# A fused attention and two-layer-MoE kernel: the first pair's q and k turned by TensorE, and the first loads and rows in another order

## The chip, the cores and the metric

The kernel runs on one core of a Trainium2 chip. A core has engines that each work through their own list of instructions in order: TensorE (PE; its weight loads are shown as PEld), VectorE (DVE), ScalarE (ACT), GpSimd (POOL) and SyncE (SP), whose list here holds nearly all the DMA issues. An instruction that waits for a semaphore holds up everything behind it on its engine. The metric is the time of one execution on the device in microseconds (us); lower is better.

## The reference

Batch 4, 8 heads, 576 rows (S), head size 64 (D); 2304 tokens in all, model width 512, hidden width 2048.

```python
scores = scale * np.matmul(q, k.transpose(0, 1, 3, 2))
thresh = np.max(scores, axis=-1, keepdims=True) - tau
scores = np.where(scores >= thresh, scores, -1e9)
attn = np.exp(scores - np.max(scores, axis=-1, keepdims=True))
attn = attn / (np.sum(attn, axis=-1, keepdims=True) + 1e-09)
x = np.matmul(attn, v)            # then heads side by side: (2304, 512)
h = x @ w_in                      # first MoE, 512 -> 2048
P = a[0] + a[1]*h + a[2]*h**2 + a[3]*h**3
Q = 1.0 + abs(b[0])*abs(h) + abs(b[1])*h**2
x = (P / (Q + 1e-6)) @ w_out      # 2048 -> 512
h = x @ w_in2                     # second MoE
g = np.where(h >= 1, h, np.where(h <= -1, 0.0, (h + 1)**2 / 4))
return g @ w_out2
```

The MoE weights come as 64-bit floats.

## The kernel before, in words

Every product is made from float16 pairs: a number is written as a high part plus a low part (`split`, L204), and a product takes three float16 matmuls. Weights come from DRAM as pairs of 32-bit words; `as_float` (L220) puts them together on DVE with three instructions of 128x1024 each (L228, L229, L230), PE finds their size (`pg`), and `split` scales them on ACT (L217), casts them on ACT (L208) and subtracts on POOL (L212). That is done in "halves": `make_half` for the 16 halves of the first MoE, whose result stays in SBUF in the chunks `wc` and is also written to `scratch`; `stage_half` for the 16 halves of the second MoE, which go to `scratch` only. The raw words of a half are the tile `rw` (two buffers, 1 MB each: `rw_0_0` is the first half of `w_in`, `rw_0_1` the first of `w_out`), the joined ones `wt` (three buffers).

Time falls into stages. First comes the **attention of batch 0** (`first_attention`), with nothing to overlap it but the halves. Heads go in four pairs. `prep_pair` loads a pair's q and k into `rqk` (one buffer), finds their size (square on ACT, `mqke` through PE, `qkr_s` on DVE), splits them into `qk`, turns `qk` by a DMA transpose into `qkT` (q and k with D and low part on the partitions), and makes `kT2`, the same k with its high and low halves crosswise, by two more DMAs from `kT`. For pairs 2 and 3 q and k are turned by one transpose each. `first_v` loads v (ten DMAs). `row_max` makes the scores once to find each row's maximum (PE `sm`, DVE `mx`, L524), cuts the maxima into three pieces (`pcs`), turns them on PE (`pmr`) and copies them to `mrow` (ACT, L560). Then nine steps for each pair (`transposed`) make the scores again, keys on the partitions, with the maximum subtracted by a third matmul (PE `st`), mark what lies under the threshold (ACT `low`, L581), subtract that on PE, take the exponential (ACT `et`, L584) and multiply by v (PE `pv`, L593). `divide` ends a pair (ACT `rd`, DVE `d` L607) and writes `xT`. The row maxima of the next pair run between the nine steps of this one.

Then the **dense steps** run: for each batch a phase of 24 steps of the first MoE and one of 24 of the second (three blocks of 192 tokens, eight chunks). `first_product` makes `ph` (L843), `rational` or `quadratic` works on it (ACT L724 to L733; DVE L726, L727, L728, L731, L737 in the first MoE; only L789 and L790 in the second), and `second_product` adds to `acc` (L857). The other halves of the second MoE and the attention of batches 1 to 3 (`attention`, row by row: PE `s`, DVE `sc` L422, `nt` L424 and `e` L384, ACT, POOL `hl`, a DMA transpose to `eT`, PE `pv` L410) are laid beside the dense steps.

The order on each engine is not the order of the code: a list scheduler places instructions by a priority and by its own reckoning of when things are ready. The code sets priorities only, with `at(when)`; unit n of 53 of `first_attention` is at `36 * n / 53 - 40`, half number k at `2.4 * k - 40`, dense step n at n, and the attention of batch 1 is spread over steps 18 to 50. A `yield` in `first_attention` ends a unit.

## Time and profile before

| | |
|---|---|
| three timed runs | 1240.43, 1245.51 (median), 1251.01 us |
| the profiled execution, its own time | 1242.5 us |
| its span, first to last instruction | 1240.7 us |
| busy over the span: PE, DVE, ACT, POOL | 88%, 79%, 68%, 44% |
| mean granted TensorE clock | 0.959 |

The shares are averages over stages with different limits; the rows further down cut the span into these stages. A group of rows gives busy time, the mean duration of one instruction, and the idle time of the engine just before, with what ended it.

### The profile page before, as it was taken

The numbers are of one execution on the slowest core, as the hardware profiler recorded it, in microseconds if no ns is written. First come the engines' busy times: TensorE is split into PE (matmuls) and PEld (weight loads), VectorE is DVE, ScalarE is ACT, GpSimd is POOL, SyncE is SP. The second block draws the span as 40 slices with busy tenths as digits, with TensorE's granted clock in tenths as the row PEclk, the third lists the DMA queues.
The fourth block names the chain that finished last, engine by engine and source line by source line (L and its number), as shares of the span: only waits on it lengthen the run. The fifth ranks groups of instructions, "written<-read, shape, count | busy, mean of one in ns | idle before, by whom it ended". The sixth has DMA issues, their size and how long they took to land.

```text
span 1240.7 us, 31727 instructions
## 1 busy us (share of the span) xinstructions
PE 1091.9 (88%) x12618; PEld 984.5 (79%) x12618; DVE 977.1 (79%) x2353; ACT 842.9 (68%) x1533; POOL 543.0 (44%) x700
## 2 busy tenths in 40 slices
PE   2787788588799999999888998998899999999998
PEld 1444455488688888899788898998788989999997
DVE  7767887899997777799997776899996768896431
ACT  2477776779785677777875776887766767775332
POOL 3424545675673556421464555223563653222221
PEclk9797898799899999999999999999999999999999
DMA  7656676734447465923596539513993478007000
GB/s 209 230 169 217 218 258 205 240 116 120 108 136 234 68 125 116 249 73 92 144 238 131 110 69 245 140 49 68 243 192 69 86 167 221 14 1 259 16 14 27
DMA packets 220341, 176.40 MB, mean 142 GB/s; under 512 B 182048, under 2 KB 193312, under 8 KB 212000
## 3 DMA queue, kind: packets, MB, share of 16 engines
q1 hardware_dynamic: 220192, 174.36, 52.7%
q8 instruction: 99, 1.62, 0.5%
q14 instruction: 50, 0.41, 0.1%
HBM read 106.83 MB, written 21.50 MB: 103 GB/s over the span
## 4 chain that ended last, share of the span: by engine, by line
PE 35%; DVE 19%; DMA 9%; ACT 6%; POOL 6%; issue 6%; SPq 1%; DVEq 0%; ACTq 0%; POOLq 0%
PE ph L843 15%; PE acc L857 15%; DMA eT<-hl 7%; POOL hl L395 3%; DVE e L384 2%; PE pv L410 2%; DVE t L731 2%; DVE t L726 2%; DVE sc L422 2%; DVE t L737 1%; DMA qkT<-qk 1%; DVE t L728 1%; POOL gg L212 1%; DVE t L727 1%; ACT hl L392 1%
## 5 line engine op out<-in xcount | busy, mean ns | idle before, releaser
L857 PE MATMUL acc<-gg,wc 128*128 128x192 f16 x4608 | 427.6, 247 | 9.8 <-POOL gg L212 6.4
L843 PEld LDWEIGHTS <-wc 128*128 128x128 f16 x4608 | 389.8, 99 | 37.4 <-issue 20.8
L857 PEld LDWEIGHTS <-wc 128*128 128x128 f16 x4608 | 383.4, 98 | 13.3 <-issue 12.0
L212 POOL TENSOR_TENSOR gg<-t,gg 128x384 f16<-128x384 f32 x192 | 193.3, 1008 | 380.0 <-ACT gg L208 330.0
L843 PE MATMUL ph<-xT,wc 128*128 128x192 f16 x2304 | 220.2, 253 | 29.7 <-DVE t L728 21.2
L843 PE MATMUL ph<-yT,wc 128*128 128x192 f16 x2304 | 215.9, 247 | 1.0 <-DVE rk_f L160 0.6
L395 POOL TENSOR_TENSOR hl<-e,hl 128x256 f16<-128x256 f32 x216 | 154.3, 735 | 0.0
L208 ACT CAST gg<-t 128x384 f16<-128x384 f32 x192 | 97.0, 508 | 68.8 <-DVE t L790 34.7
L789 DVE SCALAR_TENSOR_TENSOR t<-t,c 128x384 f32<-128x384 f32 x96 | 64.0, 667 | 77.3 <-ACT t L788 77.0
L384 DVE SCALAR_TENSOR_TENSOR e<-sc,nt,e 128x576 f32<-128x576 f32 x108 | 96.2, 891 | 31.9 <-ACT e L383 31.3
L393 POOL TENSOR_TENSOR hl<-e,hl 128x64 f16<-128x64 f32 x108 | 43.3, 401 | 145.0 <-ACT hl L392 141.4
L788 ACT ACTIVATE t<-ph,c 128x384 f32<-128x384 f32 x96 | 64.0, 667 | 51.6 <-PE ph L843 51.2
L383 ACT ACTIVATE e<-sc,nt,con 128x576 f32<-128x576 f32 x108 | 93.4, 865 | 7.4 <-POOL hl L395 1.3
L410 PE MATMUL pv<-v,eT 128*128 128x65 f16 (+3 forms) x1680 | 70.1, 194 | 26.8 <-DMA eT<-hl 26.6
L422 DVE TENSOR_SCALAR_CACHE_REDUCE sc<-s 128x576 f32<-128x576 f32 x108 | 80.9, 749 | 13.5 <-PE s L377 12.7
L410 PEld LDWEIGHTS <-eT 128*128 128x128 f16 (+1 forms) x1680 | 62.2, 100 | 36.1 <-DMA eT<-hl 33.8
L724 ACT ACTIVATE t<-ph,sc 128x384 f32<-128x384 f32 x96 | 55.2, 575 | 51.5 <-PE ph L843 50.0
L392 ACT CAST hl<-e 128x576 f16<-128x576 f32 x108 | 72.0, 668 | 25.9 <-DVE e L384 25.3
L731 DVE SCALAR_TENSOR_TENSOR t<-t,ka,t 128x384 f32<-128x384 f32 x96 | 70.1, 730 | 11.1 <-ACT t L730 10.8
L729 ACT ACTIVATE t<-t,lc 128x384 f32<-128x384 f32 x96 | 67.9, 708 | 15.4 <-DVE t L726 15.0
L212 POOL TENSOR_TENSOR wc<-wt,wc 128x256 f16<-128x256 f32 x64 | 55.3, 897 | 46.1 <-ACT wc L208 46.1
L212 POOL TENSOR_TENSOR wh<-wt,wh 128x256 f16<-128x256 f32 x64 | 59.7, 961 | 33.0 <-ACT wh L208 28.9
(231 smaller groups left out, 1901.7 us busy)
## 6 DMA issues: line engine op xcount, KB each, us to landing
wc<-scratch SPq DMA_DIRECT2D x56, 1024.0 KB, 5.8
rw<-in_moe_w_in_dram SPq DMA_DIRECT2D x16, 1024.0 KB, 5.7
rw<-in_moe_w_out_dram SPq DMA_DIRECT2D x16, 1024.0 KB, 5.1
scratch<-wc SPq DMA_DIRECT2D x8, 1024.0 KB, 5.1
scratch<-wh SPq DMA_DIRECT2D x16, 512.0 KB, 3.6
rqk<-in_q_dram SPq DMA_DIRECT2D x16, 256.0 KB, 3.6
rqk<-in_k_dram SPq DMA_DIRECT2D x16, 256.0 KB, 3.0
kT<-qkT SPq DMA_DIRECT2D x28, 144.0 KB, 2.5
```

What stands on the lines that cost most here:

```text
L208: A.copy(hi, src)
L212: G.tensor_tensor(lo[:, p], src[:, p], hi[:, p], op=ALU.subtract)
L383: A.activation(e, s, AF.Exp, bias=nb, scale=con[:, 0:1])
L384: V.scalar_tensor_tensor(e, s, th, e, op0=ALU.is_ge, op1=ALU.mult)
L392: A.copy(hi, e)
L395: G.tensor_tensor(lo_w[:, p], e[:, whole][:, p], hi[:, whole][:, p], op=ALU.subtract)
L410: T.matmul(pv[rows, 0:w], eT[:, c, cols], vv[:, h * NT + x if x < NT else H * NT + h, at : at + w], start=(n == 0), stop=(n == len(blocks) ...
L422: V.tensor_scalar(s, banks[:, 0:S], 1.0, -LARGEST, op0=ALU.mult, op1=ALU.max, accum_out=mx)
L729: A.activation(r, u, AF.Ln, bias=lc[:, 1:2], scale=lc[:, 0:1])
L731: V.scalar_tensor_tensor(s, s, ka[:, 0:1], r, op0=ALU.add, op1=ALU.mult)
L843: last = T.matmul(ph[:, f, :], w[:, wx, kt, f * P : (f + 1) * P], rhs, start=(n == 0), stop=(n == 3 * KT - 1))
L857: T.matmul(dst, w[:, wx, f, d * P : (d + 1) * P], gg[:, gx, f, :], start=(i == 0 and f == 0 and n == 0 and d % 2 == 0), stop=(i == NCH - 1 ...
```

## The change

Six edits, all in the attention of batch 0 and the first loads:

1. A new function `turned` replaces the DMA transpose and the two crosswise DMAs of pair 0. PE multiplies each of the 18 128x128 blocks of `qk` by an identity (`qk_t`, in the PSUM banks of `s`, `acc` and `ph1`); ACT copies q to `qT` and one half of k crosswise to `kT2`, DVE copies k to `kT` and the other half to `kT2`.
2. For pair 0 the low parts of q and k are made on DVE (`on_vector`) in place of POOL, and the high parts directly by ACT.
3. `tau`, `a`, `b` and the first two weight loads (`rw_0_0`, `rw_0_1`) are issued by ACT in place of SP.
4. The `mrow` copies of pair 0 go from ACT to DVE, with a PSUM bank for each.
5. Pairs 2 and 3 are prepared after the first and after the sixth step (`PREPARE`) in place of ahead of all steps.
6. The halves' priority goes from `- 40` to `- 39.5`.

```diff
--- before.py
+++ after.py
@@ -35,6 +35,7 @@
 N_TEMP, N_POLY, N_WT, N_WH, N_GG, N_ROW, N_SC = 5, 3, 3, 2, 4, 3, 2
 
 
+PREPARE = 1, 6
 ATTENTION = {1: (18, 50), 2: (60, 100), 3: (108, 147)}
 WEIGHTS = (0, 20)
 
@@ -112,11 +113,11 @@
         return sp.tile([P, n], F32, name=name, tag=f"s{n}_{tag}", bufs=4 if tag in ("mx", "nt") else 2)
 
     tau_t = small(1, "tau_t", True)
-    Q.dma_start(tau_t, tau.partition_broadcast(P))
+    A.dma_start(tau_t, tau.partition_broadcast(P))
     a_t = small(4, "a_t", True)
-    Q.dma_start(a_t, coef_a.partition_broadcast(P))
+    A.dma_start(a_t, coef_a.partition_broadcast(P))
     b_t = small(2, "b_t", True)
-    Q.dma_start(b_t, coef_b.partition_broadcast(P))
+    A.dma_start(b_t, coef_b.partition_broadcast(P))
 
 
 
@@ -238,7 +239,7 @@
         else:
             raw = rp.tile([P, NF, DM * words], raw_type, name=f"rw{m}_{i}_1", tag="rw")
             src = w_out_dram[m][i * CF : (i + 1) * CF, :].rearrange("(f p) d -> p f d", p=P)
-        Q.dma_start(raw, src)
+        (A if m == 0 and i == 0 else Q).dma_start(raw, src)
         name = f"{m}_{i}_{x}"
         src = as_float(raw.rearrange("p a b -> p (a b)"), name)
         hi, lo = dst[:, 0:E], dst[:, E : 2 * E]
@@ -314,6 +315,22 @@
                 split(to[:, :, 0:D], to[:, :, D + 1 : 2 * D + 1], raw[:, n0:n1], s_x[b], on_vector)
         return vv
 
+    def turned(qk, qT, kT, kT2):
+        last = ps_1.tile([P, 512], F32, name="qk_t8", tag="ph1")
+        for x in (1, 0):
+            most = ps_2.tile([P, 1024], F32, name=f"qk_t{x}", tag="s" if x else "acc")
+            for c in range(C):
+                dst = most[:, c * P : (c + 1) * P] if c < C - 1 else last[:, x * P : (x + 1) * P]
+                T.matmul(dst, qk[:, x, c], ident16, start=True, stop=True)
+            for src, c0, c1 in ((most, 0, C - 1), (last[:, x * P : (x + 1) * P], C - 1, C)):
+                src = src.rearrange("p (c s) -> p c s", s=P)
+                if x == 0:
+                    A.copy(qT[:, c0:c1], src)
+                else:
+                    V.tensor_copy(kT[:, c0:c1], src)
+                    A.copy(kT2[0:D, c0:c1], src[D : 2 * D])
+                    V.tensor_copy(kT2[D : 2 * D, c0:c1], src[0:D])
+
     def prep_pair(b, pr, on_vector=True):
         raws = rp.tile([P, 2, C + 1, D], F32, name=f"rqk{b}_{pr}", tag="rqk", bufs=1)
         raw = raws[:, :, 0:C, :]
@@ -340,9 +357,12 @@
             split(qk[:, x, :, 0:D], qk[:, x, :, D : 2 * D], raw[:, x], s[:, x : x + 1], on_vector)
         if b > 0 or pr < 2:
             qkT = ap.tile([P, 2 * C, P], F16, name=f"qkT{b}_{pr}", tag="qkT")
-            Q.dma_start_transpose(out=qkT, in_=qk.rearrange("p x c d -> p (x c d)"))
             qT, kT = qkT[:, 0:C], qkT[:, C : 2 * C]
             kT2 = ap.tile([P, C, P], F16, name=f"kT2{b}_{pr}", tag="kT2")
+            if b == 0 and pr == 0:
+                turned(qk, qT, kT, kT2)
+                return con, qT, kT, kT2
+            Q.dma_start_transpose(out=qkT, in_=qk.rearrange("p x c d -> p (x c d)"))
         else:
             qT, kT, kT2 = (ap.tile([P, C, P], F16, name=f"{x}{b}_{pr}", tag="eT" if pr == 2 else "hl", bufs=N_ROW)
                            for x in ("qT", "kT", "kT2"))
@@ -553,11 +573,11 @@
             V.tensor_scalar(pcs[:, x], m, 1.0 / PIECES[x], None, op0=ALU.mult)
             if x < 2:
                 V.scalar_tensor_tensor(m, pcs[:, x], -PIECES[x], m, op0=ALU.mult, op1=ALU.add)
-        for c0, c1 in ((0, NT), (NT, 2 * NT), (2 * NT, n)):
-            pm = ps_1.tile([P, 512], F32, name=f"pmr{pr}_{c0}", tag="ph0")
+        for x, (c0, c1) in enumerate(((0, NT), (NT, 2 * NT), (2 * NT, n))):
+            pm = ps_1.tile([P, 512], F32, name=f"pmr{pr}_{c0}", tag="ph0" if pr else ("ph0", "ph1", "pv")[x])
             for c in range(c0, c1):
                 T.matmul(pm[0:3, (c - c0) * P : (c - c0 + 1) * P], pcs[:, :, c], ident16, start=True, stop=True)
-            A.copy(mrow[0:3, c0 * P : c1 * P], pm[0:3, 0 : (c1 - c0) * P])
+            (A.copy if pr else V.tensor_copy)(mrow[0:3, c0 * P : c1 * P], pm[0:3, 0 : (c1 - c0) * P])
         yield
 
     def transposed(pr, ab, t, data, n):
@@ -618,7 +638,7 @@
 
     def first_attention():
 
-        pairs = [prep_pair(0, 0, False)]
+        pairs = [prep_pair(0, 0)]
         yield
         vv = first_v()
         xT[0] = [xp.tile([P, 2 * KT, TB], F16, name=f"xT0_{j}", tag="xT", bufs=NB) for j in range(NB)]
@@ -629,9 +649,6 @@
         pairs.append(prep_pair(0, 1, False))
         yield
         for _ in row_max(0, *pairs[0][1:], mrows[0]):
-            yield
-        for pr in range(2, NP):
-            pairs.append(prep_pair(0, pr, False))
             yield
         n = 0
         for pr in range(NP):
@@ -658,6 +675,9 @@
                     next(rows, None)
                 n += 1
                 yield
+                if n in PREPARE:
+                    pairs.append(prep_pair(0, len(pairs), False))
+                    yield
             for f in held:
                 f()
             divide(pr, x, d)
@@ -870,7 +890,7 @@
         with at(36 * n / N_FIRST - 40):
             next(att)
         while halves and len(halves) * N_FIRST > 2 * NCH * (N_FIRST - 1 - n):
-            with at(2.4 * (2 * NCH - len(halves)) - 40):
+            with at(2.4 * (2 * NCH - len(halves)) - 39.5):
                 i, x = halves.pop(0)
                 make_half(0, i, x, chunks[0, i], False)
```

What the scheduler makes of it, at three places. First, DVE at the start of the program, where the size of q and k (`mqke_0`) becomes the scale `qkr_0_s`. Before:

```order
L228 TENSOR_SCALAR wt_0_0_194<-rw_0_0_192 128x1024
L229 SCALAR_TENSOR_TENSOR wt_0_0_194<-rw_0_0_192,wt_0_0_194 128x1024
L230 SCALAR_TENSOR_TENSOR wt_0_0_194<-rw_0_0_192,wt_0_0_194 128x1024
L496 TENSOR_REDUCE mv_225<-v_222 128x1
L188 TENSOR_REDUCE mqke_0_166<-pmmqke_0_167 128x2
L168 TENSOR_SCALAR qkf_0_165<-mqke_0_166 128x2
L171 TENSOR_SCALAR qkf_0_165<-qkf_0_165 128x2
L496 TENSOR_REDUCE mv_225<-v_222 128x1
L172 RECIPROCAL qkr_0_s<-qkf_0_165 128x2
```

After:

```order
L229 TENSOR_SCALAR wt_0_1_334<-rw_0_1_332 128x1024
L230 SCALAR_TENSOR_TENSOR wt_0_1_334<-rw_0_1_332,wt_0_1_334 128x1024
L516 TENSOR_REDUCE mv_249<-v_246 128x1
L189 TENSOR_REDUCE mqke_0_166<-pmmqke_0_167 128x2
L231 SCALAR_TENSOR_TENSOR wt_0_1_334<-rw_0_1_332,wt_0_1_334 128x1024
L516 TENSOR_REDUCE mv_249<-v_246 128x1
L169 TENSOR_SCALAR qkf_0_165<-mqke_0_166 128x2
L255 TENSOR_REDUCE gram<-pg_0_0_222 128x1
L516 TENSOR_REDUCE mv_249<-v_246 128x1
L172 TENSOR_SCALAR qkf_0_165<-qkf_0_165 128x2
L516 TENSOR_REDUCE mv_249<-v_0_247 128x1
L173 RECIPROCAL qkr_0_s<-qkf_0_165 128x2
```

Three instructions on the first half of `w_out` (`wt_0_1`) and more of v's maxima (`mv`) now stand ahead of the scale; before, `wt_0_1` came after all of this.

Second, SP from v's last loads to the loads of pair 1 (`rqk_1`). Before:

```order
L492 DMA v_1_224<-in_v_dram 64x4x64 x2
L241 DMA rw_0_1_308<-in_moe_w_out_dram 128x2x1024
L241 DMA rw_1_0_352<-in_moe_w_in_dram 128x4x512
L343 DMA_TRANSPOSE qkT_0_187<-qk_0_162 128x18x128
L321 DMA rqk_1_265<-in_q_dram 128x2x256
L324 DMA rqk_1_265<-in_q_dram 64x64
L351 DMA kT_0_189<-qkT_0_187 64x1152
L352 DMA kT_0_189<-qkT_0_187 64x1152
L324 DMA rqk_1_265<-in_q_dram 64x64
L321 DMA rqk_1_265<-in_k_dram 128x2x256
L324 DMA rqk_1_265<-in_k_dram 64x64 x2
L241 DMA rw_1_1_394<-in_moe_w_out_dram 128x2x1024
```

After:

```order
L512 DMA v_1_248<-in_v_dram 64x4x64 x2
L242 DMA rw_1_0_376<-in_moe_w_in_dram 128x4x512
L242 DMA rw_1_1_418<-in_moe_w_out_dram 128x2x1024
L338 DMA rqk_1_289<-in_q_dram 128x2x256
L341 DMA rqk_1_289<-in_q_dram 64x64 x2
L338 DMA rqk_1_289<-in_k_dram 128x2x256
L341 DMA rqk_1_289<-in_k_dram 64x64 x2
L242 DMA rw_2_0_507<-in_moe_w_in_dram 128x4x512
L242 DMA rw_2_1_626<-in_moe_w_out_dram 128x2x1024
L365 DMA_TRANSPOSE qkT_1_322<-qk_1_297 128x18x128
```

The transpose and the crosswise DMAs of pair 0 are gone, the load of `rw_1_1` stands ahead of pair 1's loads and that of `rw_2_1` ahead of pair 1's transpose; before, `rw_2_1` stood behind pair 2's loads.

Third, DVE at the last step of the first dense phase (`t_0_2_7`), where rows of batch 1's attention (`sc`, `nt`, `e`, named by pair, group and row) are laid between. Before:

```order
L726 SCALAR_TENSOR_TENSOR t_0_2_7_4047<-t_0_2_7_4047,qc 128x384
L775 TENSOR_SCALAR c_1_5143<-w2b,iv_1_5131,rk_1_s 128x8
L727 TENSOR_TENSOR t_0_2_7_4048<-t_0_2_7_4048,ph_0_2_7_4022 128x384
L737 SCALAR_TENSOR_TENSOR t_0_2_6_3980<-t_0_2_6_3980,t_0_2_6_3981 128x384
L776 TENSOR_TENSOR c_1_5143<-c_1_5143 128x8
L728 SCALAR_TENSOR_TENSOR t_0_2_7_4048<-t_0_2_7_4048,ka_1911,ph_0_2_7_4022 128x384
L731 SCALAR_TENSOR_TENSOR t_0_2_7_4048<-t_0_2_7_4048,ka_1911,t_0_2_7_4047 128x384
L442 TENSOR_SCALAR rd_0_2_4470<-pv_0_2_4420 128x2
L443 RECIPROCAL rd_0_2_4470<-rd_0_2_4470 128x2
L789 SCALAR_TENSOR_TENSOR t_0_0_0_4262<-t_0_0_0_4262,c_0_4228 128x384
L737 SCALAR_TENSOR_TENSOR t_0_2_7_4047<-t_0_2_7_4047,t_0_2_7_4048 128x384
```

After:

```order
L442 TENSOR_SCALAR sc_1_1_2_5377,mx_1_1_2_5375<-s_1_1_2_5370 128x576
L404 SCALAR_TENSOR_TENSOR e_1_1_1_5345<-sc_1_1_1_5341,nt_1_1_1_5340,e_1_1_1_5345 128x576
L444 TENSOR_SCALAR nt_1_1_2_5376<-mx_1_1_2_5375,con_1_3965 128x1
L746 SCALAR_TENSOR_TENSOR t_0_2_7_4071<-t_0_2_7_4071,qc 128x384
L747 TENSOR_TENSOR t_0_2_7_4072<-t_0_2_7_4072,ph_0_2_7_4046 128x384
L476 TENSOR_TENSOR xT_2_3943<-xt_0_3_4858,xT_2_3943 128x128
L160 TENSOR_SCALAR rk_1_f<-g_1_5157 128x1
L442 TENSOR_SCALAR sc_1_2_0_5643,mx_1_2_0_5641<-s_1_2_0_5636 128x576
L751 SCALAR_TENSOR_TENSOR t_0_2_6_4005<-t_0_2_6_4005,ka_1935,t_0_2_6_4004 128x384
L748 SCALAR_TENSOR_TENSOR t_0_2_7_4072<-t_0_2_7_4072,ka_1935,ph_0_2_7_4046 128x384
L161 TENSOR_SCALAR rk_1_f<-rk_1_f 128x1
```

Before, seven of batch 1's 36 rows had had their `sc` here, the last of them pair 0's `sc_0_2_0`; after, it is fifteen, up to pair 1's `sc_1_1_2`. The halves go the other way: ahead of the first dense step's first DVE instruction stand the `wt` instructions of 28 and two thirds halves before, of 30 after.

## Rows read from the trace of the kernel before

**Rows 1.** Busy time by stage: stretch, its length, each engine, PEclk, DMA share, GB/s.

```profile
0.00:52.00 52.00, 20.04 (x112) 11.12 (x113) 39.04 (x101) 19.94 (x32) 18.10 (x34) 0.92 0.70 193
52.00:96.00 44.00, 37.09 (x212) 22.70 (x212) 26.37 (x67) 29.82 (x51) 13.32 (x15) 0.85 0.67 214
96.00:238.00 142.00, 107.49 (x666) 70.50 (x666) 116.68 (x240) 102.27 (x157) 76.78 (x86) 0.84 0.65 228
238.00:374.00 136.00, 112.35 (x1256) 106.31 (x1255) 131.18 (x297) 112.96 (x207) 90.40 (x92) 0.92 0.45 130
374.00:505.00 131.00, 121.87 (x1629) 112.35 (x1627) 96.21 (x260) 88.58 (x170) 67.62 (x104) 1.00 0.63 141
```

**Rows 2.** Timeline, first 60 us: start, duration, instruction, idle before and its releaser.

```profile
8.55 0.69 DVE L228 TENSOR_SCALAR wt<-rw 128x1024 int32<-128x1024 int32 x1 [1.27 <-DMA rw<-in_moe_w_in_dram]
...
12.27 0.41 DVE L188 TENSOR_REDUCE mqke<-pmmqke 128x2 f32<-128x256 f32 x1
...
13.61 0.15 DVE L172 RECIPROCAL qkr_s<-qkf 128x2 f32<-128x2 f32 x1
...
18.48 4.91 SPq L343 DMA_TRANSPOSE qkT<-qk  x1
...
28.52 1.03 PE L521 MATMUL sm<-kT,qkT 128*128 128x512 f16 x2 [1.99 <-DMA kT<-qkT]
```

**Rows 3.** The tile `rw` in the first 60 us: ns min/median/max; DMAs to landing.

```profile
L229 DVE SCALAR_TENSOR_TENSOR wt<-rw,wt x6: 1215/1233/1573, 9.3 to 58.2; 128x1024 int32<-128x1024 int32 x6
...
DMA to landing us min/median/max: 5.2/6.7/8.9
```

**Rows 4.** Busy time in two stretches of the first loads, columns as in rows 1.

```profile
6.00:8.00 2.00, 0.00 (x0) 0.00 (x0) 1.17 (x11) 0.20 (x1) 0.00 (x0) 1.00 1.05 396
12.00:14.00 2.00, 1.03 (x9) 0.74 (x7) 1.93 (x8) 0.14 (x1) 0.00 (x0) 1.00 0.90 203
```

**Rows 5.** Timelines of DVE and of ACT, columns as in rows 2.

```profile
43.91 0.18 DVE L553 TENSOR_SCALAR pcs<-mx 128x9 f16<-128x9 f32 x1
...
57.23 0.69 DVE L228 TENSOR_SCALAR wt<-rw 128x1024 int32<-128x1024 int32 x1 [3.50 <-DMA rw<-in_moe_w_out_dram]
...
51.81 1.35 ACT L581 ACTIVATE low<-st,con 128x576 bf16<-128x576 f32 x2
...
238.74 0.58 ACT L724 ACTIVATE t<-ph,sc 128x384 f32<-128x384 f32 x1 [0.79 <-PE ph L843]
```

**Rows 6.** Groups of instructions, 0 to 240 us: count | busy us, mean ns | idle before.

```profile
L230 DVE SCALAR_TENSOR_TENSOR wt<-rw,wt 128x1024 int32<-128x1024 int32 x28 | 38.6, 1378 | 0.3
L229 DVE SCALAR_TENSOR_TENSOR wt<-rw,wt 128x1024 int32<-128x1024 int32 x29 | 37.8, 1304 | 0.5
...
L228 DVE TENSOR_SCALAR wt<-rw 128x1024 int32<-128x1024 int32 x29 | 22.2, 764 | 15.9 <-POOL wc L212 5.2 <-POOL wh L212 4.7 <-DMA rw<-in_moe_w_out_dram 4.5
L524 DVE TENSOR_REDUCE mx<-sm 128x1 f32<-128x512 f32 x32 | 21.9, 686 | 12.0 <-PE sm L521 11.6
...
L208 ACT CAST wc<-wt 128x1024 f16<-128x1024 f32 x16 | 16.5, 1038 | 0.1
```

**Rows 7.** DVE's groups in the first dense phase, 238 to 374 us.

```profile
L384 DVE SCALAR_TENSOR_TENSOR e<-sc,nt,e 128x576 f32<-128x576 f32 x7 | 6.4, 910 | 0.1
...
L422 DVE TENSOR_SCALAR_CACHE_REDUCE sc<-s 128x576 f32<-128x576 f32 x7 | 5.2, 742 | 0.0
...
L215 DVE SCALAR_TENSOR_TENSOR qk<-rqk,qkr_s,qk 128x576 f16<-128x576 f32 x4 | 4.3, 1086 | 0.0
```

**Rows 8.** The second dense phase, 374 to 505 us: PE's groups.

```profile
L843 PE MATMUL ph<-yT,wc 128*128 128x192 f16 x549 | 52.4, 246 | 0.0
L857 PE MATMUL acc<-gg,wc 128*128 128x192 f16 x528 | 50.4, 246 | 0.0
L410 PE MATMUL pv<-v,eT 128*128 128x65 f16 x198 | 13.4, 193 | 7.9 <-DMA eT<-hl 7.9
```

**Rows 9.** The chain that ended last, 374 to 520 us: start, us, piece.

```profile
385.84 1.98 PE acc L857 x24
```

## The prediction

> **What bounds the kernel now.** I read the span first (1240.7 us, table above), then the busy times by stage [rows 1]; the reader should see that the limit changes. From 374 us on PE is busy 93% of the time and granted its full clock: there a microsecond of PE work costs nearly a microsecond. In the first dense phase, 238 to 374 us, DVE is busy 131.2 of 136.0 us (96%) and PE 112.4: DVE sets the pace. In the 238 us ahead of it, batch 0's attention, no engine is full: DVE is busy 182.1 us (39.0 + 26.4 + 116.7), PE 164.6, ACT 152.0, so that a chain through several engines decides, and whoever stands in a queue behind something slow. The change works directly on this first part only; its second effect is that the scheduler lays the rest out anew.
>
> The start reads from the timeline [rows 2]: the scale of q and k is there at 13.76 us, the DMA transpose is issued at 18.48 and takes 4.91 us of SP's list, and k's crosswise copy is there at 28.52, when the first complete scores can run. Then come the row maxima until `pcs` at 44.09, and the first `low` of pair 0 at 51.81 [rows 5]. Pair 0 ends on DVE at 96, where the second stage of [rows 1] is cut, and the first dense `ph` reaches ACT at 238.74 [rows 5].
>
> My sum is made against the profiled execution: span 1240.7, own time 1242.5 us. That is 3.0 under the median of the three runs, 1245.5; the step between the two goes in at the end.
>
> **Part 1: the start, up to the first `low`.** ACT now issues `tau`, `a`, `b` and the first `w_in` load behind its table load, by my estimate 1.3 us later than SP did, so DVE begins on it at 9.85 and not 8.55 [rows 2] and is through at 13.0 or so. ACT issues the first `w_out` load only when q has landed and been squared; q goes out first on SP, so I estimate an issue at 7.2. These loads took 5.2 to 8.9 us to land, 6.7 in the middle [rows 3]: landing at 13.9. DVE now has this half's first two instructions ahead of `mqke`. From 13.9: 0.69 + 1.22 (L228 and L229 while POOL is quiet [rows 2, 3]), 0.68 for a maximum of v (the 128x512 reduction [rows 6]), 0.41 for `mqke` [rows 2] make 16.9; then 1.22, three maxima of v (2.0), `gram` 0.42 and small ones 0.5 until the scale is out at 21.1. That is **7.3 us later** than 13.76.
>
> From the scale to crosswise k it was 14.8 us. Now: small instructions and v's last maxima 1.8, q's low part 0.9, small ones 0.5, k's low part 0.9 (a 128x576 instruction of this kind, 0.910 [rows 7]), which makes 25.2. PE's 18 products fit beside this (eight `pg` products of this size took about 1 us). On DVE then: 1.0 until the first conversion instruction of the next half is done, half a microsecond for v's maximum through PE, 1.22, and the copy of k out of PSUM. No such DVE copy is in the trace; the bounds are 1.04 (ACT's cast of 128x1024 [rows 6]) and 1.37 (twice the 128x512 reduction out of PSUM, 0.686 [rows 6]), and I take 1.3. With its tail 0.4, one more conversion 1.22, and the crosswise copy 1.3 + 0.3, it ends at 32.5, against 28.5: **4.0 later**. So the stretch that the change attacks is 3.4 us shorter, and the new order ahead of it takes back twice as much.
>
> The row maxima keep their 15.6 us (the DVE instructions in the new order add up to 15.4): `pcs` at 47.9. From there to `low` it took 7.7 us, since the three `mrow` copies shared one bank and stood in ACT's list between weight casts. On DVE with a bank each: PE 0.6, three copies 0.57 + 0.57 + 0.25, others between 0.4, last products 0.7: 3.1. First `low` at 51.0: **0.8 earlier**; 2.3 earlier if the `w_out` load lands in 5.2 us, 1.4 later with 8.9.
>
> A row of the first loads shows what could hold that load up: from 12 to 14 us the DMA engines are 90% busy at 203 GB/s, with v's small pieces; from 6 to 8, with large ones, they move 396 GB/s [rows 4]. At these rates q and k need 2.6 us, `w_in` 2.7, v 5.2 and `w_out` 2.7; if nothing else holds them and they begin at 3.1, all are through at 16.3, and a `w_out` load that shares evenly with v lands only there: the first `low` is then 2.4 us later than in my sum, 1.6 after the old one.
>
> The Trainium skill, "DMA: Bandwidth & Descriptors", section "Issuing engines are not separate DMA queues", speaks against this edit: DMAs run on the same 16 engines whichever engine starts them, and only the issue time is saved. The rule is this sharing, and the sum by it would be that of the paragraph above; rows from two engines that issue at once are not in this trace.
>
> **Part 2: pair 0, 51.8 to 95.95.** DVE was busy 26.4 of 44.0 us, PE 37.1, ACT 29.8 [rows 1]. Of DVE's 17.6 us of idle time, 3.50 went to a `w_out` load that SP had issued late, behind pair 2's loads [rows 5]; this load now stands ahead of pair 1's transpose, so that this goes. Pair 3's preparation (4.4 us of ACT, 1.7 of DVE) leaves the stretch. In comes one and a third halves more: three DVE instructions of 0.764, 1.304 and 1.378 [rows 6] and some 0.9 of small ones are 4.35 a half, 5.8 us, in what was idle time, and 2 us on PE. I take **-3.0**: bounds +2 (DVE's surplus shows) and -7 (5.8 less 1.7 more DVE work, 30.5 us, at the 82% of the next stretch is 37).
>
> **Part 3: 96 to 238 us.** The halves are the same number (20 and two thirds), the row maxima too; pair 3's preparation comes in: **+1.5** of DVE's 1.7.
>
> So the first dense step comes at 236.4, or 2.3 us earlier.
>
> **Part 4: the first dense phase.** By the order, by its last step 15 rows of batch 1's attention have had their `sc` and 14 their `e`, against 7 and 7. A row costs DVE 0.742 + 0.910 [rows 7] and about 0.3 of small ones, 1.95. Added: 8 x 0.742 + 7 x 0.910 + 8 x 0.3 = 14.7, two `qk` of 1.09 [rows 7], and about 2 of the ends of rows; removed: 5.8, the halves already made. That is 13.1, at 96% busy with nowhere to hide: **+13**.
>
> **Part 5: the second dense phase.** The same eight rows are missing here. 24 products take 1.98 us [rows 9]; the trace shows 1077 of them [rows 8], 88.9 us of PE's 121.9, and the other 33 are some 22 rows, 1.5 us each. Eight rows less: **-12**, since PE is the bound; at least nothing, if the rows' own chain is: PE sat idle 7.9 us there for `eT` [rows 8]. The later phases keep nearly the same order: 0.
>
> The sum: -0.8 - 3.0 + 1.5 + 13 - 12 = **-1.3 us**: 1241 on the profiled execution, 1244 on the median.
>
> **The rivals.** *What is pulled ahead is not given back.* The eight rows cost 13 us where DVE is full, and the second phase ends when batch 1's last row is through, not when PE is. Worked out: -2.3 + 13 = +10.7, 1256; with a late load (+2.2) and no gain in part 2 (+3) 1261. With those two it decides as soon as less than 3.5 of the 12 us come back. For it: PE's idle time for `eT`; against it: PE was idle for 9.1 of 131 us there, so work removed must show. Slower by over 1%: 0.18.
>
> *The queues were the real limit.* With no transposes of pair 0 in SP's list and the weight loads ahead of the pairs' loads, DVE's 56 us of idle time in the first 238 us shrink: part 1 at -2.3, part 2 at -7, and the 142 us of the third stretch, with 118.4 us of DVE work, at 90% busy instead of 82%: 131.5, -10.5; with +1 of parts 4 and 5 that is -18.8 at most, 1227, and half of it in part 3 gives 1232. For it: 4.5 us of waits for `w_out` loads [rows 6]; against it: PE's slower clock there, 0.84 [rows 1], and longer waits for PE's scores, 11.6 us [rows 6]. Faster by over 1%: 0.22.
>
> *It doesn't do what it says:* the first `low` comes no earlier, because DVE stands longer before the `w_out` load that shares the DMA engines with v. Landing at 16.3 (or, after 8.9 us, at 16.1) it costs 2.4, 1246.5. For it: the engines' 90% in [rows 4]; against it: the median of 6.7 [rows 3]. Chance 0.15, inside 1%. It is also what follows from the rule of the Trainium skill, "DMA: Bandwidth & Descriptors", section "Issuing engines are not separate DMA queues".
>
> **How the numbers follow.** Within 1% (12.4 us, about what a measurement of this kernel can tell from no change): 0.60, of which 0.45 the forecast and 0.15 the last rival; faster 0.22, slower 0.18. The range reaches 14 us to each side: it leaves out the ends of the first two rivals, a tenth each way.
>
> **What would show it.** In the trace after: DVE idle at 13 to 14 us for the `w_out` load ahead of `mqke`; the scale at about 21 us and not 14; the first `low` near 51; no DVE wait of 3.5 us for `w_out` in pair 0; the first dense ACT instruction at about 236; the first dense phase some 13 us longer at the same DVE share, the second some 12 shorter. I am wrong if the first dense step moves by more than 6 us, or the two phases don't make up for each other.

## The result, and the profile after

The changed kernel takes 1235.24 us (median of 13 executions) against 1245.81 for the kernel before (13 executions): 0.9908 of its time, with a 95% interval of 0.9884 to 0.9931. That is some 11 us. It lies within the range, 9 us under the forecast, and just inside the 1% that I had called no change, though the interval reaches beyond that 1%.

The profiled execution of the changed kernel took 1239.17 us (span 1237.1), 3.9 above its median; that of before, 1242.5, lies 3.3 below its own. So the two traces differ by 3.6 us of span where the medians differ by 10.6, and what follows is read by stage. First the busy times by stage of the changed kernel, in the stretches and columns of [rows 1]:

```profile
0.00:52.00 52.00, 24.04 (x144) 14.50 (x145) 44.37 (x110) 21.83 (x33) 16.73 (x33) 0.97 0.66 198
52.00:96.00 44.00, 32.61 (x205) 21.37 (x204) 35.28 (x83) 30.84 (x53) 21.07 (x21) 0.85 0.77 246
96.00:238.00 142.00, 116.24 (x732) 77.16 (x730) 118.31 (x245) 105.51 (x162) 75.41 (x87) 0.84 0.68 236
238.00:374.00 136.00, 113.76 (x1309) 105.17 (x1307) 132.19 (x317) 117.74 (x224) 90.02 (x101) 0.94 0.48 119
374.00:505.00 131.00, 124.41 (x1630) 117.35 (x1629) 86.84 (x233) 79.88 (x156) 66.42 (x94) 0.99 0.63 144
```

DVE is busy 79.7 of the first 96 us, against 65.4 in [rows 1]. The timeline of the changed kernel says what became of the steps (start, duration, instruction, idle time before it and its releaser), as in [rows 2] and [rows 5]; lines have moved by 1 to 20:

```profile
6.95 0.39 ACTq L242 DMA_DIRECT2D rw<-in_moe_w_out_dram  x1
...
13.81 0.69 DVE L229 TENSOR_SCALAR wt<-rw 128x1024 int32<-128x1024 int32 x1 [0.58 <-DMA rw<-in_moe_w_out_dram]
...
16.28 0.41 DVE L189 TENSOR_REDUCE mqke<-pmmqke 128x2 f32<-128x256 f32 x1
...
19.99 0.15 DVE L173 RECIPROCAL qkr_s<-qkf 128x2 f32<-128x2 f32 x1
...
22.39 1.04 PE L324 MATMUL qk_t<-fixed,qk 128*128 128x128 f16 x8 [2.72 <-DVE qk L216]
...
28.52 1.42 DVE L332 CAST kT<-qk_t 64x1024 f16<-64x1024 f32 x2
...
29.79 0.59 PE L541 MATMUL sm<-kT,qkT 128*128 128x512 f16 x1 [2.54 <-DVE kT L332]
...
43.77 0.18 DVE L573 TENSOR_SCALAR pcs<-mx 128x9 f16<-128x9 f32 x1
...
47.18 1.37 ACT L601 ACTIVATE low<-st,con 128x576 bf16<-128x576 f32 x2 [0.73 <-PE st L598]
...
85.97 0.75 DVE L627 SCALAR_TENSOR_TENSOR d<-d,rd 128x576 f32<-128x576 f32 x1
...
92.59 0.17 DVE L573 TENSOR_SCALAR pcs<-mx 128x9 f16<-128x9 f32 x1
...
99.57 1.35 ACT L601 ACTIVATE low<-st,con 128x576 bf16<-128x576 f32 x2
...
232.19 0.58 ACT L744 ACTIVATE t<-ph,sc 128x384 f32<-128x384 f32 x1 [0.52 <-PE ph L863]
```

Steps of the kernel before that answer to these and were not shown yet are the last `pcs` of pair 1, the first division of pair 0, the last of pair 1's three `mrow` copies, and pair 1's first `low`.

```profile
89.00 0.17 DVE L553 TENSOR_SCALAR pcs<-mx 128x9 f16<-128x9 f32 x1
...
95.95 0.76 DVE L607 SCALAR_TENSOR_TENSOR d<-d,rd 128x576 f32<-128x576 f32 x1 [3.48 <-ACT rd L606]
...
99.22 0.25 ACT L560 CAST mrow<-pmr 3x128 f16<-3x128 f32 x1
99.38 1.35 ACT L581 ACTIVATE low<-st,con 128x576 bf16<-128x576 f32 x2
```

The reader is to see three things. The first `low` is 4.6 us earlier (47.18 against 51.81) and pair 0's division 10.0 (85.97 against 95.95). Pair 1's first `low` is not earlier at all (99.57 against 99.38). And the first dense step is 6.5 us earlier (232.19 against 238.74 in [rows 5]). So a gain of ten microseconds is there at 86 us and is gone at 99.6; 6.5 us are there again at the first dense step.

What was done in that time is in the busy times, cut at pair 1's first `low` and at the first dense step. Before:

```profile
0.00:99.40 99.40, 57.99 (x326) 34.09 (x327) 68.33 (x169) 53.16 (x87) 34.82 (x51) 0.88 0.69 202
99.40:238.70 139.30, 107.33 (x668) 70.86 (x668) 114.42 (x238) 98.87 (x153) 74.05 (x84) 0.84 0.65 229
```

After:

```profile
0.00:99.60 99.60, 60.25 (x364) 38.03 (x365) 80.49 (x196) 56.26 (x91) 40.80 (x57) 0.90 0.71 217
99.60:232.20 132.60, 108.42 (x669) 71.26 (x668) 111.75 (x231) 97.66 (x151) 68.60 (x80) 0.85 0.69 241
```

In the same 99.5 us DVE does 12.2 us more work. Part of it is the change's own: two low parts of 0.81, two pairs of copies of 1.42 and 1.55 of `mrow` copies, 6.0 us. Most of the rest is weights: 30 `wt` conversions in 34.73 us, against 24 in 29.13, which is 10 halves after and 8 before. From there both kernels go at the same pace: 139.3 us for 20.67 halves before, 132.6 for 19.67 after, 6.74 us a half in both. **By the time pair 1 begins, two more halves are made.** At that pace they would be worth 13.5 us: one of them was cashed as 6.5 us at the first dense step, the other stands ahead of it (29.67 halves against 28.67). That a half is worth this is not shown. Over all 14 kernels below the same stretch takes 6.72 to 7.57 us a half, and the kernel with the copies on ACT, with the same 10 halves ahead of the stretch and 19.67 in it, takes 145.8 us for it, with DVE idle for 32 us of them, against 21 in the changed kernel.

The first dense phase then takes 143.9 us against 135.4, the second 127.9 against 137.9 (the second phase is counted from its first instruction on DVE, L789 before and L809 after), so that batch 1's first dense step comes at 504.0 in place of 512.1, 8.1 earlier. The remaining 733.1 us were 728.6 before; the last run below shows what such a difference between two traces is worth.

### The profile page after: what moved, and what is told of

Its sections match the earlier page's. It is cut to its first block, busy times and chain, and to the rows that moved or that the text cites. A ratio compares the mean times of both kernels' runs of the same rounds, so it can differ in the third digit from the quotient of the medians.

```text
span 1237.1 us, 31750 instructions
## 1 busy us (share of the span) xinstructions
PE 1095.3 (89%) x12636; PEld 988.4 (80%) x12636; DVE 979.3 (79%) x2362; ACT 839.5 (68%) x1532; POOL 542.7 (44%) x698
## 4 chain that ended last, share of the span: by engine, by line
PE 40%; DVE 24%; DMA 11%; POOL 9%; issue 9%; ACT 6%; SPq 1%; DVEq 0%; ACTq 0%; POOLq 0%
PE acc L877 15%; PE ph L863 15%; DMA eT<-hl 8%; POOL hl L415 3%; PE pv L613 2%; PE pv L430 2%; DVE t L746 2%; POOL wh L213 2%; DVE e L404 2%; DVE t L751 2%; DVE sc L442 2%; POOL gg L213 1%; DVE t L757 1%; DVE t L748 1%; DVE t L747 1%
## 5 line engine op out<-in xcount | busy, mean ns | idle before, releaser
L863 PE MATMUL ph<-yT,wc 128*128 128x192 f16 x2304 | 213.4, 246 | 3.7 <-DVE t L748 2.5
L415 POOL TENSOR_TENSOR hl<-e,hl 128x256 f16<-128x256 f32 x216 | 160.6, 764 | 0.0
L209 ACT CAST gg<-t 128x384 f16<-128x384 f32 x192 | 96.9, 508 | 75.1 <-DVE t L810 36.8
L809 DVE SCALAR_TENSOR_TENSOR t<-t,c 128x384 f32<-128x384 f32 x96 | 66.2, 690 | 88.9 <-ACT t L808 87.0
L404 DVE SCALAR_TENSOR_TENSOR e<-sc,nt,e 128x576 f32<-128x576 f32 x108 | 97.5, 903 | 28.1 <-ACT e L403 27.9
```

Source lines behind the costliest of these rows:

```text
L209: A.copy(hi, src)
L404: V.scalar_tensor_tensor(e, s, th, e, op0=ALU.is_ge, op1=ALU.mult)
L415: G.tensor_tensor(lo_w[:, p], e[:, whole][:, p], hi[:, whole][:, p], op=ALU.subtract)
L863: last = T.matmul(ph[:, f, :], w[:, wx, kt, f * P : (f + 1) * P], rhs, start=(n == 0), stop=(n == 3 * KT - 1))
```

## The experiments

Four kernels have one part of the change each, four lack one, four test reasons. All numbers of the traces are from one execution each; a ratio is to the kernel before, with its 95% interval. "Halves" counts the `wt` conversions begun by the first dense step, in thirds; "phases" is the length of batch 0's two dense phases, "rest" what follows them to the end of the span.

| kernel | ratio | first low of pair 0 | of pair 1 | first dense step | halves | phases | batch 1's start | rest |
|---|---|---|---|---|---|---|---|---|
| before | 1 | 51.8 | 99.4 | 238.7 | 28.67 | 273.4 | 512.1 | 728.6 |
| changed | 0.9908 | 47.2 | 99.6 | 232.2 | 29.67 | 271.8 | 504.0 | 733.1 |
| edits 1, 2 alone | 0.9976 | 48.8 | 94.0 | 232.4 | 28.00 | 279.0 | 511.4 | 733.1 |
| edit 3 alone | 1.0111 | 53.7 | 96.9 | 246.3 | 28.00 | 278.9 | 525.2 | 738.9 |
| edit 4 alone | 0.9962 | 51.4 | 87.1 | 224.6 | 26.67 | 279.4 | 504.0 | 736.6 |
| edits 5, 6 alone | 1.0074 | 52.0 | 104.2 | 249.5 | 31.67 | 271.1 | 520.6 | 730.4 |
| without 5, 6 | 1.0059 | 47.0 | 95.0 | 233.8 | 28.33 | 276.7 | 510.5 | 737.5 |
| without 3 | 1.0001 | 47.3 | 96.5 | 230.2 | 29.67 | 275.0 | 505.2 | 737.2 |
| without 4 | 0.9963 | 48.7 | 97.8 | 236.0 | 30.00 | 269.4 | 505.4 | 731.4 |
| without 1, 2 | 0.9998 | 47.8 | 95.8 | 234.2 | 29.00 | 276.7 | 510.9 | 736.0 |
| edits 1, 2, 4 alone | 1.0088 | 47.1 | 91.4 | 236.1 | 27.33 | 283.6 | 519.7 | 735.1 |
| mrow in one bank | 0.9981 | 47.2 | 88.7 | 222.3 | 27.00 | 287.2 | 509.5 | 735.2 |
| copies on ACT | 1.0019 | 49.0 | 95.3 | 241.2 | 29.67 | 270.6 | 511.8 | 738.7 |
| later window | 0.9912 | 46.6 | 99.3 | 231.5 | 29.67 | 267.8 | 499.3 | 734.8 |

Edit 6 has no run of its own. In the changed kernel, and in it without edit 5, it does nothing: the program with 40 is that with 39.5, instruction for instruction. But where SP issues the first loads it does act. With edits 5 and 6 alone, and without edit 3, q and k are issued ahead of the first `w_in` load (in both kernels q at 2.12 and `w_in` at 5.65 us; before, `w_in` at 2.12 and q at 2.60), and the scale comes earlier than the 13.61 us of [rows 2]. These are its rows in the two kernels:

```profile
10.25 0.17 DVE L173 RECIPROCAL qkr_s<-qkf 128x2 f32<-128x2 f32 x1
...
10.47 0.17 DVE L173 RECIPROCAL qkr_s<-qkf 128x2 f32<-128x2 f32 x1
```

So the run of edits 5 and 6 alone does not show edit 5 alone, and the run without edit 3 does not have the first loads as they were before.

**One part each.** Edits 1 and 2 (`turned`, `prep_pair(0, 0)`):

> The kernel before with edits 1 and 2 alone (pair 0's q and k turned by TensorE products, low parts on DVE). Theory O, order: what is won ahead of pair 0 and in it is hidden, since pair 1's first low waits for its own mrow and not for pair 0's end (99.4 and 99.6 us in the two traces, though pair 0's first division instruction came at 95.95 and 85.97); this edit alone then changes the median by -3 to +2 us, and pair 1's first low stays within 2 us of 99.4. Theory S, start: the start carries through, and since the turn is the largest edit there it gives at least half of the gain, -5 to -8 us, with pair 1's first low at 95 or earlier.

Measured 0.9976 (0.9953 to 1.0000). Pair 1's first `low` did move, to 94.0, and the first dense step to 232.4, which is theory S's place; the time moved by some 3 us (the interval is 0 to 5.9), which is nearer to theory O's.

Edit 3:

```diff
-    Q.dma_start(tau_t, tau.partition_broadcast(P))
+    A.dma_start(tau_t, tau.partition_broadcast(P))
...
-        Q.dma_start(raw, src)
+        (A if m == 0 and i == 0 else Q).dma_start(raw, src)
```

> The kernel before with edit 3 alone (tau, a, b and the first two weight loads issued by ACT). Theory O: within 3 us of the kernel before. Theory Q, queues (the weight loads' places in SP's list were the limit): the gain shows here, -5 us or more, with the DVE wait of 3.5 us for the w_out load in pair 0 gone; if that wait stays, it was not this edit that removed it.

Measured 1.0111 (1.0072 to 1.0150): slower by some 14 us, so theories O and Q both fall. DVE's wait of 3.50 us for `w_out` is gone, but a wait of 0.91 for `w_in` stands there, and the scale at 20.3 us now comes ahead of a DMA transpose.

Edit 4:

```diff
-            pm = ps_1.tile([P, 512], F32, name=f"pmr{pr}_{c0}", tag="ph0")
+            pm = ps_1.tile([P, 512], F32, name=f"pmr{pr}_{c0}", tag="ph0" if pr else ("ph0", "ph1", "pv")[x])
...
-            A.copy(mrow[0:3, c0 * P : c1 * P], pm[0:3, 0 : (c1 - c0) * P])
+            (A.copy if pr else V.tensor_copy)(mrow[0:3, c0 * P : c1 * P], pm[0:3, 0 : (c1 - c0) * P])
```

> The kernel before with edit 4 alone (pair 0's mrow copies on DVE, a PSUM bank each). All theories: the step from the last pcs to the first low falls from 7.7 us to about 3.3, so the first low comes at 47 to 48 in place of 51.8. Theory O: none of these 4 us is left at pair 1's first low (97.5 to 101), and the time is within 3 us of before. Theory S: -3 to -4 us at the end.

Measured 0.9962 (0.9935 to 0.9990). The step that all theories shared failed: the first `low` came at 51.4. The timeline of this kernel shows why (DVE and ACT):

```profile
46.03 0.87 DVE L560 CAST mrow<-pmr 3x512 f16<-3x512 f32 x2
...
49.83 0.68 ACT L328 ACTIVATE qk<-rqk 128x576 f16<-128x576 f32 x1 [1.59 <-DMA rqk<-in_q_dram]
...
50.51 1.03 ACT L208 CAST wc<-wt 128x1024 f16<-128x1024 f32 x1
...
51.44 1.36 ACT L581 ACTIVATE low<-st,con 128x576 bf16<-128x576 f32 x2
```

`mrow` is complete at 46.9, but `low` stands in ACT's list behind the square of pair 2's q, which waits for its load, and behind a weight cast. A wait was removed and the next one in the list took its place. Pair 1's first `low` then came 12 us earlier, and the first dense step 14 (with two halves fewer); 8 us of it were still there at batch 1's start, and 3.4 at the end, which is theory S's time; theory O's place for pair 1 (97.5 to 101) was missed.

Edits 5 and 6:

> The kernel before with edits 5 and 6 alone (pairs 2 and 3 prepared after the first and the sixth step; priority 39.5). Theory O: nearly the whole gain is here, -7 to -12 us, with the first dense step some 6 us earlier. Theory S: within 3 us of before. By the order on DVE 31 and two thirds halves stand ahead of the first dense step (28 and two thirds before) and 15 rows of batch 1 by the last step of the first dense phase (7 before), so the first dense phase should be 8 to 13 us longer and the second 10 to 12 shorter, whichever theory holds.

Measured 1.0074 (1.0045 to 1.0103): slower by some 9 us, so neither theory holds, although its dense phases came as expected (142.3 and 128.8 us; 135.4 and 137.9 before). No part alone brings the gain of all; the best, edit 4, brings 0.4%.

**One part undone.** The diffs are those above, backwards.

> The changed kernel (median 1235.2) with edits 5 and 6 alone undone: pairs 2 and 3 are prepared ahead of all steps again and the priority is 40. Alone these edits cost 9.4 us. Additive theory (each edit has its own price): without them the kernel is 9 us faster than the changed one, 1226. Interaction theory (the preparations must stand behind the first steps only when pair 0 starts early, so that they fill a wait that is otherwise DVE's idle time ahead of pair 1): 1238 to 1246, with DVE idle for 48 us or more ahead of the first dense step (39.9 in the changed kernel, 55.9 before).

> The changed kernel with edit 3 alone undone: tau, a, b and all weight loads issued by SP. Alone this edit cost 15.8 us. Additive theory: 15 us faster than the changed kernel, 1220. Interaction theory: the load costs only where the DMA transpose waits behind a late scale; with the turn on TensorE the later scale (20.0 against 13.6 us) is paid back by a half that is converted before it, so undoing it leaves the time within 4 us of 1235.

> The changed kernel with edit 4 alone undone: pair 0's mrow copies go through one PSUM bank on ACT again. Alone the edit gained 3.4 us. Additive theory: 1238 to 1239, the first low some 4 us later (51). Hidden theory (what is won ahead of pair 1 is lost before pair 1's mrow): the same time, 1233 to 1237, with pair 1's first low within 2 us of 99.6.

> The changed kernel with edits 1 and 2 alone undone: pair 0 is turned by the DMA transpose again. Alone the edit gained 0.8 us (interval 0 to 5.9). Additive theory: 1236, within 4 us of the changed kernel. Interaction theory: with the loads on ACT the scale is late (20 us), the transpose then takes its 4.9 us of SP's list behind it and the first low comes at 54 or later, as with the loads alone; 1250 or more.

Measured 1.0059, 1.0001, 0.9963 and 0.9998, against 0.9908 for the whole: without any one part the kernel is slower than the changed one, by 0.6% to 1.5%, and no interval touches that of the changed kernel. Edit 4's is the nearest (from 0.9933, against 0.9931), and the last kernel below, as fast as the changed one, has an interval up to 0.9940: that edit 4 is needed is not clear of the noise. The additive theory is refuted: the four parts alone come to -0.2%, +1.1%, -0.4% and +0.7%, +1.2% together, and the whole to -0.9%. The parts that cost time alone, edit 3 and edits 5 and 6, are missed in company; for edit 6 a reason is seen: it acts where SP issues the first loads and does nothing in the changed kernel. But the medians, 1252.5, 1244.4, 1240.7 and 1245.0 us, do not lie where a theory of mine had put them either; only edit 4's is near one (additive, 1238 to 1239), and its first `low` came at 48.7 and not 51. Without edits 1 and 2 the scale is late (19.6 us) and the transpose stands behind it, as I had said, yet the first `low` comes at 47.8 and not at 54 or later. DVE was idle 44.2 us ahead of the first dense step without edit 5, less than the 48 I had expected (233.8 of span less 189.55 of work). Undoing edit 3 left the first dense step and batch 1's start where they were within 2 us (230.2 and 505.2), so that its 9 us are not lost in the stages that I had argued about.

With edits 5 and 6 on the one hand and the other four on the other, four of these kernels make a square. Their first `low` of pair 1 comes at 99.4 before, 104.2 with edits 5 and 6, 95.0 with the others, 99.6 with all. Edits 5 and 6 cost 4.8 and 4.6 there, the others gain 4.4 and 4.6: up to here the parts add up, although edit 6 moves the first loads in one of the two pairs and not in the other. The halves begun by then are 8, 10.33, 8 and 10. At the pace from there to the first dense step (139.3 us for 20.67 halves, 145.3 for 21.33, 138.8 for 20.33, 132.6 for 19.67: 6.74 to 6.83 each), edits 5 and 6 lay two halves ahead of pair 1 for 4.7 us that would cost 13.5 later. The other ten kernels do not all keep that pace, so this is an account of these four and not a price. The parts stop adding up in how many more halves the new order puts ahead of the dense steps: with edits 5 and 6 alone 31.67 in all, three more than before, which is 20 us at that pace and shortens the dense phases by 2; with all edits one more.

**Reasons tested.** The changed kernel with the `mrow` of every pair in one bank and on DVE:

```diff
-            pm = ps_1.tile([P, 512], F32, name=f"pmr{pr}_{c0}", tag="ph0" if pr else ("ph0", "ph1", "pv")[x])
+        pm = ps_1.tile([P, 512], F32, name=f"pmr{pr}", tag="ph0")
...
+            r = slice(32 * x, 32 * x + 3)
...
-            (A.copy if pr else V.tensor_copy)(mrow[0:3, c0 * P : c1 * P], pm[0:3, 0 : (c1 - c0) * P])
+            V.tensor_copy(mrow[0:3, c0 * P : c1 * P], pm[r, 0 : (c1 - c0) * P])
```

> The changed kernel with the maxima of every pair, not of pair 0 alone, turned into one PSUM bank (three groups of partitions) and copied to mrow by DVE. Hidden theory (pair 1's first low waits for mrow, whose three copies stand in ACT's list between weight casts): the step from a pair's last pcs to its first low falls from 7.0 us (pair 1) to 3 to 4, pair 1's first low comes at 95 to 97 and some 2 to 3 us are won at each of pairs 1 to 3, the first dense step 6 us or more earlier (at 27 halves ahead of it in place of 30, up to 15 us earlier); at the end 1226 to 1233. Rival (DVE's own list is the limit, and three more copies of 0.7 us a pair on it cost what they win): 1234 to 1242.

Measured 0.9981 (0.9956 to 1.0006), median 1245.3, outside both ranges. Locally it does what it should: pair 1's `low` follows the last `pcs` by 4.1 us (84.57 to 88.65) where it was 7.0, so that some 3 us of pair 1's wait there were these copies'. The last `pcs` itself comes 8 us earlier than in the changed kernel (84.57 against 92.59), and the first dense step at 222.3. But only 27 halves are made by then, and the two dense phases pay for it, 287.2 us against 271.8. The windows of its two dense phases show how:

```profile
222.30:366.50 144.20, 111.15 (x1225) 104.34 (x1223) 139.81 (x287) 112.43 (x200) 88.42 (x92) 0.92 0.40 127
366.50:509.50 143.00, 131.50 (x1757) 118.96 (x1756) 105.18 (x294) 97.90 (x191) 81.61 (x120) 1.00 0.73 153
```

DVE is full in the first (97%), and 4 of batch 1's `e` rows are done in it where the changed kernel has 14: its attention slips into the second, where PE has 131.5 us to do in place of 121.3. An early first dense step is not a gain by itself.

All crosswise copies of pair 0 on ACT:

```diff
-                    V.tensor_copy(kT[:, c0:c1], src)
+                    A.copy(kT[:, c0:c1], src)
...
-                    V.tensor_copy(kT2[D : 2 * D, c0:c1], src[0:D])
+                    A.copy(kT2[D : 2 * D, c0:c1], src[0:D])
```

> The changed kernel with all crosswise copies of pair 0's k on ACT, in place of DVE for kT and half of kT2. DVE theory (up to pcs DVE works through a list of four halves, ten maxima and the rest, whatever the scale is; pcs came at 43.0 to 46.5 in ten kernels with the scale at 10.3 to 20.6): 2.8 us less on DVE's list, so pcs comes 1.5 to 3 us earlier, at 41 to 42.3, even though the first complete scores come later than 29.8. Chain theory (the chain scale, turn, copies, scores, maxima sets pcs): four copies one behind the other on ACT take 1 to 2 us longer, so pcs comes at 45 to 46. At the end within 5 us of 1235 by either.

Measured 1.0019 (0.9992 to 1.0046), median 1250.5, worse than the changed kernel and far from the 1235 that both theories had. Neither theory holds: the complete scores came earlier (27.84) and not later, and the last `pcs` at 44.76, near the chain theory's place but for another reason. DVE had 2.8 us less to do, yet its last maximum came only 0.35 us earlier (40.66 against 41.01): it waited 2.20 us for the first complete scores instead. And the last `pcs` came 1 us later than in the changed kernel, because of something else, told at the end.

Edits 1, 2 and 4 without the others:

> The kernel before with edits 1, 2 and 4 (TensorE turns pair 0, mrow on DVE with a bank each), without the loads on ACT and without the new places of the preparations. Alone the two gave -0.8 and -3.4 us. Additive theory: 1241 to 1243. Start theory (the two belong together, since the turn without quick mrow copies leaves its gain in the wait for mrow): first low at 47 or earlier, 1235 to 1238, and the loads and the places of the preparations then gave nothing of their own.

Measured 1.0088 (1.0057 to 1.0120): slower, although the first `low` came at 47.1, where the start theory had it. Both theories fall.

One number that no edit touches:

```diff
-ATTENTION = {1: (18, 50), 2: (60, 100), 3: (108, 147)}
+ATTENTION = {1: (18, 50), 2: (62, 100), 3: (108, 147)}
```

> The changed kernel with one number changed that has nothing to do with the six edits: the attention of batch 2 is spread over dense steps 62 to 100 in place of 60 to 100. The order on DVE is the same, apart from buffer names, up to the middle of batch 1's first dense phase (some 550 us), and no work is added or taken away. Layout theory (the later phases, which no edit touches, move by several us by the place of the attention rows alone): the first 504 us as before and the time 3 to 8 us away from 1235.2, probably above it. Rival (the rest of the program is the same whatever the order, and its differences are those between executions): 1233.5 to 1237.

Measured 0.9912 (0.9884 to 0.9940), median 1235.55: the same as the changed kernel, so that here another order behind 550 us cost nothing, and the layout theory falls in this form and the rival's range holds. The run shows a second thing. Up to 550 us its order is that of the changed kernel, but its batch 1 began at 499.3 us in place of 504.0: two executions of the same order differ by 4.7 us in the first 500. At pair 1's first `low` they differ by 0.3 and at the first dense step by 0.7, so the earlier columns of the table are firmer than the later ones. A late difference of that size between two traces, such as the 4.5 us of the rest, shows nothing by itself.

## Why the prediction was right or wrong

**The start: the scale was right, what follows from it was not.** The late `w_out` load landed at 13.8 (13.9 forecast), the scale was there at 20.1 (21.1), the complete scores at 29.8 (32.5). The step that failed is "the row maxima keep their 15.6 us": they began 1.3 us later than before and ended at the same time, the last `pcs` done at 43.95 against 44.09 and 47.9 forecast. I had added a delay to a stretch that had room for it. In the 14 kernels the first complete scores come at 21.7 to 33.6 us and the last `pcs` at 43.0 to 46.5 all the same; with the scores at 33.6 (edit 3 alone) only 11.8 us are left between the two and with 21.7 (without edit 3) it is 21.5. What fills the room is in DVE's list, four halves in every one of these kernels; that DVE's work alone sets the end is not so, as the copies on ACT showed. From the end of `pcs` to `low` it took 3.2 us, as forecast (3.1), in the changed kernel; edit 4 alone does not give that (7.2). So the first `low` came 4.6 us earlier, and not 0.8.

**Pair 0:** from the first `low` to the division 38.8 us against 44.1, -5.3, where I took -3.0 and bounds of +2 and -7. But that the gain goes on to the next pair was an assumption behind the sum, and it is wrong: 13.6 us lie between this division and pair 1's `low`, against 3.4 before, and what `low` waits for in both kernels is the last of pair 1's `mrow` copies. Pair 1's last `pcs`, which comes ahead of them, is 3.6 us later than before (92.59 against 89.00), behind more work on DVE. Pair 3's preparation, which I had moved behind 96 us, still lies ahead of pair 1's `low` (q's square begins at 84.25, its scale is out at 91.27 us). On ACT the three `mrow` copies of pair 1, which edit 4 leaves there, stand at 95.5, 98.0 and 99.4 between weight casts:

```profile
95.53 0.58 ACT L580 CAST mrow<-pmr 3x512 f16<-3x512 f32 x1
...
98.00 0.56 ACT L580 CAST mrow<-pmr 3x512 f16<-3x512 f32 x1
98.47 1.04 ACT L209 CAST wc<-wt 128x1024 f16<-128x1024 f32 x1
99.42 0.25 ACT L580 CAST mrow<-pmr 3x128 f16<-3x128 f32 x1
```

**96 to 238 us:** I had the same number of halves there, and +1.5. It was one fewer from pair 1 on, since two more were ahead of it; from pair 1's `low` to the first dense step it took 6.7 us less, where I had 1.5 more. Together, the first dense step moved by 6.5 us and not by 2.3, more than the 6 us that I had named as the point from which the account is wrong. By that the account of the first 238 us is wrong. That the time lies in the range is owed to the range, 14 us to each side, and not to the sum, which had -1.3 us for some -11; up to batch 1's start the traces show -8.1.

**The dense phases** were right in mechanism and a third too large in size: +8.5 for +13 in the first, DVE at 97%; -10.0 for -12 in the second, where eight rows less come to 1.25 us each and not 1.5. The first phase was charged 13.1 us of DVE work, and DVE was busy 140.0 us in it against 130.5, +9.5. The trace has the rows: 14 `e` and 16 `sc` where [rows 7] has seven each. They make up for each other to 1.5 us, as forecast (+1). That a pulled-ahead row is not given back, the first rival, did not happen.

**The rival that came nearest** is the one on DVE's idle time: it shrank from 55.9 to 39.9 us ahead of the first dense step, of which the waits for `sm`, 11.6 us in [rows 6], lost half:

```profile
L544 DVE TENSOR_REDUCE mx<-sm 128x1 f32<-128x512 f32 x32 | 21.7, 683 | 5.8 <-PE sm L541 5.6
```

But its reason, the queues and the places of the weight loads, is not shown: edit 3 alone makes the kernel slower, and without it DVE is idle less still (230.2 us of span less 195.7 of work, 34.6). Nor did the waits for weight loads go: of 6.1 us (4.5 for `w_out`, 1.6 for `w_in`) 4.3 are left, 3.7 of them now for `w_in`.

**The shared DMA engines:** the load of `w_out` landed in 6.8 us, as the median had it, so this rival's price was not paid at the `low`. (Its 2.6 and 5.2 us for q with k and for v are the 203 GB/s of [rows 4] raised from a share of 90% to a full one; at 203 they would be 2.9 and 5.8.) The sharing itself is there, on v's side. One of v's issues held SP for 3184 ns in the changed kernel, where before none took over 630, and v's loads took 4.3 us to land in the middle and 7.2 at most, against 2.9 and 4.1. Before and after:

```profile
L490 SPq DMA_DIRECT2D v<-in_v_dram x8: 552/628/630, 6.5 to 12.5; - x8
...
DMA to landing us min/median/max: 2.4/2.9/4.1
L510 SPq DMA_DIRECT2D v<-in_v_dram x8: 602/630/3184, 7.0 to 15.1; - x8
...
DMA to landing us min/median/max: 2.4/4.3/7.2
```

The rule of the Trainium skill, "DMA: Bandwidth & Descriptors", section "Issuing engines are not separate DMA queues", that DMAs issued by several engines run on the same 16 and only the issue time is saved, agrees with this. A second issuer is not needed for it: without edit 3, where SP itself issues the load of `w_in` just ahead of v, one of v's issues also held SP for 1922 ns, and v took 3.7 us to land in the middle and 5.5 at most. What the sharing costs had to be looked for at the transfer that was moved past, not at the one that was moved.

**What stays open.** Where the changed kernel's 11 us come from is not shown as a whole: 6.5 us are there at the first dense step and 8.1 at batch 1's start, in traces that differ by several us from their medians. Why each part alone, and the whole without one, loses up to 21 us in the stages between pair 1 and batch 1's start, or behind it, is not settled: every edit lays all engines' lists anew, and the runs show that the halves ahead of the first dense step explain a part of it (from 27 to some 30 halves the two dense phases fall from 287 us to 268 to 275, at 31.67 they take 271; at 26.67, with edit 4 alone, 279, which does not fit), not which instruction stands in the way. Undoing edit 3 costs 0.9% without moving batch 1's start; where is not shown.

## What to carry to other kernels

Ahead of a stage that has room, a time won is not a time kept: ask which instruction of the next stage waits last, and whether the scheduler will fill the room with other work, and count that work in units (here halves) beside the microseconds. Where a scheduler lays the lists anew, prices of single edits need not add up: here one part (edits 5 and 6) cost 0.7% alone and its loss cost 1.5% in company, so test a part by leaving it out as well as by itself. And two traces of one execution each cannot settle 5 us of 1240.
